# Single 32-bit matmuls in place of three half-precision passes, in three stages of a spectral filter

## The chip, the cores and the metric

The kernel runs on one core of one Trainium2 chip. The metric is the device time of one execution, in microseconds (us). The engines are TensorE (PE in the profile; its weight loads are listed apart as PEld), VectorE (DVE), ScalarE (ACT), GpSimd (POOL) and SyncE (SP), which here issues all DMAs.

## The reference

```python
x = A_x                                        # 1 x 2048 x 512, float32
xn = layernorm(x)                              # over the 512
X = rfft2(xn) * (w_r + 1j * w_i)               # 2048 x 257
s = irfft2(X, (2048, 512))
gate, up = xn @ W_gate, xn @ W_up              # 512 x 1376 each
h = gate * (gate > 0) * up
g = silu(h @ W_down)                           # 1376 x 512
return x + s * g
```

Two branches share the normalised input: a two-dimensional spectral filter, and a gated feed-forward network whose result multiplies the filter's.

## The kernel before

**Numbers in halves.** TensorE is fed in half precision. To keep the accuracy, each float32 operand is split in two fp16 numbers: a high half, written by a copy (mostly ScalarE), and a low half, the float32 value less the high half (a subtraction on VectorE). A product is then three passes into the same PSUM accumulator, high x high, high x low and low x high; `PASSES = ((0, 0), (0, 1), (1, 0))` lists the pairs. Constants are split on the host by `_half`.

**The feed-forward branch.** The 2048 rows are handled in four blocks of 512 (numbered 0 to 3), the 1376 hidden columns in eleven tiles of 128 (the last has 96), numbered `f` = 0 to 10. Gate and up product are `gu{block}_{f}_{0|1}`: four parts of the contraction by three passes, 12 matmuls of 512 columns each. `r`, `h32` and `h16` are the rectified gate, the product and its halves; `dn` are the down products, matmuls of `h16` with the scaled down weights `wds`, also in three passes, into four accumulators per block. The weights are scaled to powers of two on the chip. For gate and up that goes by groups of tiles: `squares` sums the weights' squares into `m{g}`, a small 32-bit matmul `sum{g}` with a matrix of ones (lines 507 to 515) adds them over the partitions, and VectorE makes the scales `p{g}` and their inverses `rho`. For the down weights, `down_scale` (579 to 599) multiplies `md`, the sums of absolute values in each row of a tile, with `rho`, so it needs the inverses of all seven groups, reduces them, and hands them to `greatest` (561 to 569): one DMA writes the 128 values, one per partition, to DRAM (`row_md`), a second spreads them to all partitions (`rows_md`), VectorE takes the maximum `max_md`, and five small operations (`pd`, `cdi`, `scd`) make the scales. `down_weights` (601 to 608) then writes the high half of each `wds` on ScalarE and the low half on VectorE. The filter's weights go through the same chain as `mw`.

**The filter branch.** The transform over the 512 columns is a set of folds on VectorE (sums and differences of mirrored columns, result `xs`) with matmuls by the constants `cD`; that over the 2048 rows is factored in 64 x 32. There are eight chunks of the work, and these TensorE stages:

- *First stage*, one step `s1_c` for each of the eight row chunks (`first_stage`, 462 to 484): products of the folded input `xs` with 64 x 64 matrices `cR`. Four 64 x 64 tiles of the array work side by side (two blocks of rows by two of columns). Columns 0 to 256 use one matrix and 257 to 511 another (`RANGES`), so a step is 2 ranges x 3 passes x 4 tiles = 24 matmuls. Ahead of it, `split` (454 to 460) makes the halves `xs16`. Behind it, ScalarE and VectorE write the result's halves `t1` in two pieces (448 and 64 columns) and SP stores them in DRAM (`A_d`).
- *Middle*, for each of eight chunks `q` of frequencies (`fft_chunk`, 775 to 932): `y` (64-row matmuls with the chunk's matrices `cm`), `x` (with `cD`), the multiplication by the filter on VectorE and GpSimd, `z` (with `cD`) and `v`, the inverse with 64 x 64 matrices, here called the inverse 16-point stage. `v_stage` (914 to 925) has 3 passes x 4 tiles of 512 columns; chunk 0 has three more matmuls of 255 columns with the correction matrices `cX`. Its input is split in halves in `z16`, its output in `t9`, which goes to DRAM (`C_d`).
- *Last stage*, one step `s2_c` for each of eight chunks (`last_stage`, 935 to 982): `cR[2 + m]` times the rows of `C_d`, with tiles and ranges as in the first stage, then unfolding, the product with the gate `g`, the addition of `x` and the store.

**What sets the order.** Nothing is issued as it is written. Every piece of work is a `step` (101 to 118) with an engine, a planned cost, the names that it reads and writes, and perhaps a due time. `Plan.run` (120 to 207) plays these steps through with the planned costs: on each engine it takes, among the steps that could begin about then, the one with the earliest due time. It counts buffers of each pool and a planned lag after each engine, and on TensorE it prefers steps of the same array shape (`mode`). The order in which the steps begin in this plan becomes each engine's order of instructions, fixed at build time; on the chip, semaphores hold an instruction until its inputs are there. Planned costs of the three stages are `SCOST` (first and last) and `VCOST` (inverse), line 38:

```python
YCOST, VCOST, SCOST, MODE, JOIN = 0.63, 0.59, 0.6, 0.095, 21.31
```

The small sums `sum2` to `sum6`, the accumulators of `s1`, `s2`, `y`, `x`, `z` and `v` all share one PSUM tag, `F`, of two buffers, so a third step must wait until the readers of the first are done. Nearly every operation passes through the wrapper `InOrder` (line 65), so rows of the profile carry L65 and are told apart by tile names.

Of the kernel before, what the change touches and what calls it, by code (L numbers as in the profile page):

```python
# [14 lines left out]
P = 128  # L15
# [22 lines left out]
YCOST, VCOST, SCOST, MODE, JOIN = 0.63, 0.59, 0.6, 0.095, 21.31  # L38
# [196 lines left out]
def kernel(ctx: ExitStack, tc: tile.TileContext, x, wg, wu, wd, wl, ew, sp, c_r, c_d, c_m, c_x, c_s, out):  # L235
# [12 lines left out]
    C_d = dram.tile([N1, N2, 2 * D], F16, name="C_d")  # L248
# [205 lines left out]
    def split(c):  # L454
        tile_of(f"xs16_{c}", "k4", [P, 2, 2, D], F16)
        x16, xs = (lambda: T[f"xs16_{c}"]), (lambda: T[f"xs{c}"])
        parts = [(f"xs{c}", i) for i in range(6)]
        step("ACT", act(1024), lambda: ACT.activation(x16()[:, :, 0, :], xs(), AF.Copy), reads=parts, writes=[(f"xs16_{c}", 0)])
        step("DVE", dve(1024), lambda: DVE.tensor_sub(x16()[:, :, 1, :], xs(), x16()[:, :, 0, :]),
             reads=[*parts, (f"xs16_{c}", 0)], writes=[(f"xs16_{c}", 1)], port=True)  # L460

    def first_stage(c, due):
        tile_of(f"s1_{c}", "F", [P, 2, D], F32)
        tile_of(f"t1_{c}", "k4", [P, 2, 2, D], F16)
        ps, t1 = (lambda: T[f"s1_{c}"]), (lambda: T[f"t1_{c}"])

        def run():
            x16 = T[f"xs16_{c}"]
# [6 lines left out]
        step("PE", SCOST, run, mode=1, reads=["cR", (f"xs16_{c}", 0), (f"xs16_{c}", 1)], writes=[f"s1_{c}"], due=due, margin=MARGIN)  # L475
# [299 lines left out]
    def fft_chunk(q, due):  # L775
        a16n, xsn, pfn, pon, p16n, z16n, t9n, atn, wtn = (f"{k}_{q}" for k in ("a16", "xsp", "pf", "po", "p16", "z16", "t9", "at", "wt"))
        for n, tag, shape, dtype in ((atn, "k4", [P, 2, 2, D], F16), (f"cm{q}", "k2", [P, 2, 2, 2, 64], F16),
# [5 lines left out]
                                     (z16n, "k4", [P, 2, 2, D], F16), (f"v{q}", "F", [P, 2, D], F32),  # L783
                                     (t9n, "k4", [P, 2, 2, D], F16), *((f"tt{i}_{q}", "k2", [P, 16, 32], F32) for i in range(4))):
# [21 lines left out]
        def y_stage():  # L806
            y = T[f"y{q}"]
            for b in range(2):
                for t in range(4):
                    for n, (h, l) in enumerate(PASSES):  # L810
                        for g in range(2):
# [5 lines left out]
                            matmul(y[:, g, t, b, :], at()[rows, b, h, t * P:(t + 1) * P], cm()[rows, b, 0, l, :], start=n == 0, stop=n == 2)  # L817
# [92 lines left out]
        step("ACT", act(1024), lambda: ACT.activation(z16()[:, 0], zv(), AF.Copy), reads=[f"z{q}"], writes=[(z16n, 0)])  # L910
        step("DVE", dve(1024), lambda: DVE.tensor_sub(z16()[:, 1], zv(), z16()[:, 0]), reads=[f"z{q}", (z16n, 0)], writes=[(z16n, 1)])


        def v_stage():
            v = T[f"v{q}"]
            for n, (h, l) in enumerate(PASSES):
                if n == 2 and q == 0:
                    lo, hi, _ = RANGES[1]
                    for h1, l1 in PASSES:
                        matmul(v[0:64, 0, lo:hi], cX[:, 1, h1, :], z16()[0:64, l1, 0, lo:hi], start=False, stop=False)  # L920
                for b in range(2):
                    for t in range(2):
                        at = slice(64 * t, 64 * t + 64)
                        matmul(v[64 * b:64 * b + 64, t, :], cm()[at, b, 1, h, :], z16()[at, l, b, :], start=n == 0, stop=n == 2)
        step("PE", VCOST, v_stage, mode=1, reads=[(z16n, 0), (z16n, 1), f"cm{q}", "cX"], writes=[f"v{q}"], due=due[3], margin=MARGIN)
        t9 = lambda: T[t9n]
        step("ACT", act(1024), lambda: ACT.activation(t9()[:, :, 0, :], T[f"v{q}"], AF.Copy), reads=[f"v{q}"], writes=[(t9n, 0)], due=due[3] + 4)
        step("DVE", dve(1024), lambda: DVE.tensor_sub(t9()[:, :, 1, :], T[f"v{q}"], t9()[:, :, 0, :]), reads=[f"v{q}", (t9n, 0)], writes=[(t9n, 1)], due=due[3] + 6)
        for b in range(2):
            step("SP", .6, lambda b=b: SP.dma_start(C_d[8 * q + 4 * b:8 * q + 4 * b + 4].rearrange("(t o) n x -> (o n) t x", t=2),  # L930
                                                     t9()[64 * b:64 * b + 64].rearrange("m t h d -> m t (h d)")),
                 reads=[(t9n, 0), (t9n, 1)], writes=[("C_d", q, b)], kb=256)


    def last_stage(c, due):
        ctn, zn, aen, yen, sn = (f"{k}{c}" for k in ("ct", "zz", "ae", "ye", "sv"))
        for n, tag, shape, dtype in ((ctn, "k4", [P, 2, 2, D], F16), (f"s2_{c}", "F", [P, 2, D], F32), (zn, "k4", [P, 2, D], F32),
                                     (aen, "k2", [P, 2, 2, 130], F32), (yen, "k4", [P, 2, 2, 258], F32), (sn, "k4", [P, 2, D], F32)):
            tile_of(n, tag, shape, dtype)
        for i in range(2):  # L940
            step("SP", .6, lambda i=i: SP.dma_start(T[ctn][64 * i:64 * i + 64].rearrange("s e h d -> s e (h d)"), C_r[2 * c + i]),
                 reads=[("C_d", q, b) for q in range(NCH) for b in range(2)], writes=[(ctn, i)], lead=14, kb=256)

        def run():
            for a, b, m in RANGES:
                for n, (h, l) in enumerate(PASSES):
                    for i in range(2):
                        rows = slice(64 * i, 64 * i + 64)
                        for e in range(2):
                            matmul(T[f"s2_{c}"][64 * e:64 * e + 64, i, a:b], cR[rows, 2 + m, h, :], T[ctn][rows, e, l, a:b], start=n == 0, stop=n == 2)  # L950
# [50 lines left out]
    step("SP", .6, lambda: SP.dma_start(cX, c_x), writes=["cX"], lead=20, kb=128)  # L1001
# [75 lines left out]

def _constants():
# [49 lines left out]
    c_m = _half(m2.transpose(0, 2, 1, 3, 4))  # L1128
    c_x = _half(np.stack([dM.reshape(N1, N1), dMi.reshape(N1, N1)], axis=1))
# [17 lines left out]
    return np.tile(_half(R.transpose(1, 0, 2)), (2, 1, 1, 1)), _half(dd), c_m, c_x, c_s, ks_of  # L1147
# [42 lines left out]
```

## Time and profile before

| | |
|---|---|
| device time, median of 3 runs | 408.8 us (408.79 to 408.81) |
| the profiled execution's own span | 407.1 us, 7606 instructions |
| TensorE busy | 401.4 us, 2992 matmul records |
| weight loads | 211.5 us |
| VectorE busy | 304.0 us |
| ScalarE busy | 188.0 us |
| GpSimd busy | 46.7 us |
| DMA | 51.78 MB, mean 127 GB/s |

The span is the time from the profile's first instruction to its last; the device time also has the little that lies around it. In a row, names such as `s<-xs,cR` give the written and the read tiles without their buffer numbers; `x48` counts instructions; a shape such as `64*64` ahead of the operands is the part of the array that a matmul uses. A wait row gives the waiting engine and tile, the engine and tile waited for, the total in us and the number of waits.

### The profile page before, as it was taken

To read this page: it belongs to the slowest core of one execution; us is meant where nothing else is said; L and a number is where in the kernel's file an instruction comes from. 1 tells how busy PE (TensorE), PEld (TensorE's weight loads), DVE (VectorE), ACT (ScalarE), POOL (GpSimd) and SP (SyncE) were. 2 spreads that over 40 slices of the span, in tenths; PEclk is the share of its full clock that TensorE was granted. 3 is DMA by queue.
4 is the path that set the end of the run, shared out by engine and by line. 5 is a ranking of instruction groups with operands and counts; after the bars stand their busy time and mean duration, and the time that the engine had idled before them with its cause. 6 is when DMAs were issued, how large, how long until landed. Compare 5 with 4: busy or idle time off the path is not lost.

```text
span 407.1 us, 7606 instructions
## 1 busy us (share of the span) xinstructions
PE 401.4 (99%) x2992; PEld 211.5 (52%) x2992; DVE 304.0 (75%) x647; ACT 188.0 (46%) x358; POOL 46.7 (11%) x72
## 2 busy tenths in 40 slices
PE   8999999999999999999999999999999999999995
PEld 7864444444444445455465455546555444444555
DVE  4897986998798979706987578686792328987974
ACT  4999823743467636222355433534523336242411
POOL 0000000000000000001612032030330008040300
PEclk9999999999999999999999999999999999999999
DMA  7980002218549608690006540324201297563242
GB/s 244 403 304 1 0 2 109 54 52 208 171 152 305 172 15 209 128 291 13 2 0 191 173 144 0 100 92 149 52 2 52 61 242 182 161 185 105 103 156 103
DMA packets 36291, 51.78 MB, mean 127 GB/s; under 512 B 15840, under 2 KB 17600, under 8 KB 36256
## 3 DMA queue, kind: packets, MB, share of 16 engines
q1 hardware_dynamic: 36256, 51.31, 42.5%
q8 instruction: 23, 0.38, 0.4%
q14 instruction: 12, 0.10, 0.1%
HBM read 35.55 MB, written 12.60 MB: 118 GB/s over the span
## 4 chain that ended last, share of the span: by engine, by line
PE 97%; ACT 1%; DVE 1%; issue 0%
PE gu L65 55%; PE dn L65 27%; PE s L65 3%; PE z L65 3%; PE xx L65 3%; PE small L65 2%; PE y L65 2%; PE v L65 2%; PE dn_3b L65 1%; ACT xT L65 1%; ACT wgu L65 0%; PE head L65 0%; DVE xT L65 0%; PE sum L65 0%; DVE p L65 0%
## 5 line engine op out<-in xcount | busy, mean ns | idle before, releaser
L65 PE MATMUL gu<-xT,wgu 128*128 128x512 f16 (+1 forms) x1008 | 213.3, 369 | 0.4 <-DVE xT L65 0.4
L65 PEld LDWEIGHTS <-wgu 128*128 128x128 f16 x1008 | 97.5, 98 | 107.5 <-issue 3.5
L65 PE MATMUL dn<-wds,h 128*128 128x512 f16 (+2 forms) x528 | 115.8, 373 | 0.0
L65 PEld LDWEIGHTS <-h 128*128 128x128 f16 (+1 forms) x561 | 53.7, 98 | 57.3 <-issue 2.0
L65 DVE TENSOR_TENSOR h<-gu,r 128x512 f32<-128x512 f32 (+2 forms) x52 | 33.6, 646 | 24.2 <-PE gu L65 22.9
L65 ACT ACTIVATE h<-h 128x512 f16<-128x512 f32 (+1 forms) x44 | 27.5, 626 | 51.0 <-DVE h L65 51.0
L65 POOL TENSOR_TENSOR po<-tt,tt 128x256 f32<-128x256 f32 x16 | 14.4, 900 | 262.6 <-DVE tt L65 208.7
L65 ACT ACTIVATE r<-gu 128x512 f32<-128x512 f32 (+1 forms) x44 | 26.2, 595 | 36.5 <-PE gu L65 36.3
L65 DVE TENSOR_TENSOR h<-h,h 128x512 f16<-128x512 f32 (+1 forms) x44 | 29.7, 689 | 5.3 <-ACT h L65 5.1
L65 DVE SCALAR_TENSOR_TENSOR tt<-xsp,cw,wt 128x512 f32<-128x512 f32 x32 | 25.3, 847 | 0.0
L65 POOL TENSOR_TENSOR ae<-zz 128x128 f32<-128x128 f32 (+1 forms) x32 | 17.8, 593 | 62.8 <-ACT zz L65 47.9
L65 ACT ACTIVATE g<-dn,cdi 128x512 f32<-128x512 f32 (+1 forms) x16 | 10.6, 673 | 23.9 <-PE dn L65 23.9
L65 PE MATMUL gu<-xT,wgt 128*64 128x256 f16 (+1 forms) x144 | 17.0, 309 | 0.0
L65 DVE TENSOR_TENSOR sv<-sv,g 128x512 f32<-128x512 f32 (+1 forms) x17 | 11.2, 690 | 6.4 <-ACT g L65 6.1
L65 DVE TENSOR_TENSOR t<-v,t 128x1024 f16<-128x1024 f32 x8 | 9.8, 1219 | 7.9 <-ACT t L65 7.9
L65 DVE TENSOR_TENSOR z<-z,z 128x1024 f16<-128x1024 f32 x8 | 9.7, 1218 | 7.5 <-ACT z L65 7.5
L65 ACT ACTIVATE z<-z 128x1024 f16<-128x1024 f32 x8 | 8.2, 1024 | 15.2 <-PE z L65 15.2
L65 POOL TENSOR_TENSOR pf<-tt,tt 128x256 f32<-128x256 f32 x16 | 14.0, 888 | 7.7 <-PE gu L65 7.7
L65 ACT ACTIVATE p<-pf 128x1024 f16<-128x1024 f32 x8 | 8.4, 1056 | 13.0 <-DVE pf L65 13.0
L65 DVE SCALAR_TENSOR_TENSOR wgu<-raw,p,wgu 128x512 f16<-128x512 f32 x20 | 14.4, 745 | 0.1
L65 ACT ACTIVATE xs<-xs 128x1024 f16<-128x1024 f32 x8 | 8.3, 1052 | 12.8 <-DVE xs L65 9.3
L65 ACT ACTIVATE wgu<-raw 128x512 f16<-128x512 f32 x20 | 12.3, 619 | 3.7 <-DMA raw<-in_wg 3.7
(134 smaller groups left out, 430.6 us busy)
## 6 DMA issues: line engine op xcount, KB each, us to landing
A_d<-t SPq DMA_DIRECT2D x16, 256.0 KB, 3.3
rw<-in_wl SPq DMA_DIRECT2D x8, 512.0 KB, 5.1
wt<-in_wl SPq DMA_DIRECT2D x8, 512.0 KB, 4.8
at<-A_d SPq DMA_DIRECT2D x8, 512.0 KB, 4.9
C_d<-t SPq DMA_DIRECT2D x16, 256.0 KB, 3.3
ct<-C_d SPq DMA_DIRECT2D x16, 256.0 KB, 5.6
xt<-in_x SPq DMA_DIRECT2D x16, 256.0 KB, 4.3
out<-xt SPq DMA_DIRECT2D x15, 256.0 KB, 2.1
```

The costliest lines, as they stand in the source:

```text
L65: return lambda *args, **kw: self.tc.keep_in_program_order(f(*args, **kw))
```

## The change

In the first, the inverse and the last stage, each product of three fp16 passes becomes one matmul with float32 operands. The constants `cR` are kept in float32 (one 64 x 64 matrix, 256 bytes a row, in place of two halves), and `cm` and `cX` as well, except that the half of each which the forward stage `y` uses still holds packed fp16 halves, read through a bitcast view. The inputs are no longer split: `split` returns at once and the first stage reads `xs`; `z16` and `t9` are float32 copies from PSUM, without the subtraction for a low half, and `C_d` in DRAM holds one float32 in place of two fp16. The forward intermediate `A_d` and all other products stay in halves. The planned costs of the three stages are set to .82 and .80.

```diff
-YCOST, VCOST, SCOST, MODE, JOIN = 0.63, 0.59, 0.6, 0.095, 21.31
+YCOST, VCOST, SCOST, MODE, JOIN = 0.63, 0.8, 0.82, 0.095, 21.31
...
-    C_d = dram.tile([N1, N2, 2 * D], F16, name="C_d")
+    C_d = dram.tile([N1, N2, D], F32, name="C_d")
...
-    cR = cpool.tile([P, 4, 2, N1], F16, name="cR")
+    cR = cpool.tile([P, 4, N1], F32, name="cR")
...
-    cX = cpool.tile([64, 2, 2, 64], F16, name="cX")
+    cXf = cpool.tile([64, 2, 64], F32, name="cX")
+    cX = cXf.bitcast(F16).rearrange("p a (h x) -> p a h x", h=2)
...
     def split(c):
-        tile_of(f"xs16_{c}", "k4", [P, 2, 2, D], F16)
+        return
...
             for a, b, m in RANGES:
-                for n, (h, l) in enumerate(PASSES):
-                    for e in range(2):
-                        rows = slice(64 * e, 64 * e + 64)
-                        for i in range(2):
-                            matmul(ps()[64 * i:64 * i + 64, e, a:b], cR[rows, m, h, :], x16[rows, i, l, a:b], start=n == 0, stop=n == 2)
+                for e in range(2):
+                    rows = slice(64 * e, 64 * e + 64)
+                    for i in range(2):
+                        matmul(ps()[64 * i:64 * i + 64, e, a:b], cR[rows, m, :], xs[rows, i, a:b], start=True, stop=True)
...
-                            matmul(y[:, g, t, b, :], at()[rows, b, h, t * P:(t + 1) * P], cm()[rows, b, 0, l, :], start=n == 0, stop=n == 2)
+                            matmul(y[:, g, t, b, :], at()[rows, b, h, t * P:(t + 1) * P], cm()[:, b, 0].bitcast(F16)[rows, 64 * l:64 * l + 64], start=n == 0, stop=n == 2)
...
-        step("ACT", act(1024), lambda: ACT.activation(z16()[:, 0], zv(), AF.Copy), reads=[f"z{q}"], writes=[(z16n, 0)])
-        step("DVE", dve(1024), lambda: DVE.tensor_sub(z16()[:, 1], zv(), z16()[:, 0]), reads=[f"z{q}", (z16n, 0)], writes=[(z16n, 1)])
+        step("ACT", act(1024), lambda: ACT.activation(z16(), zv(), AF.Copy), reads=[f"z{q}"], writes=[(z16n, 0)])
...
+            for b in range(2):
+                for t in range(2):
+                    at = slice(64 * t, 64 * t + 64)
+                    matmul(v[64 * b:64 * b + 64, t, :], cm()[at, b, 1, :], z16()[at, b, :], start=True, stop=bool(q or t or b))
+                    if q == t == b == 0:
+                        lo, hi, _ = RANGES[1]
+                        matmul(v[0:64, 0, lo:hi], cXf[:, 1, :], z16()[0:64, 0, lo:hi], start=False, stop=True)
...
-        step("ACT", act(1024), lambda: ACT.activation(t9()[:, :, 0, :], T[f"v{q}"], AF.Copy), reads=[f"v{q}"], writes=[(t9n, 0)], due=due[3] + 4)
-        step("DVE", dve(1024), lambda: DVE.tensor_sub(t9()[:, :, 1, :], T[f"v{q}"], t9()[:, :, 0, :]), reads=[f"v{q}", (t9n, 0)], writes=[(t9n, 1)], due=due[3] + 6)
+        step("ACT", act(1024), lambda: ACT.activation(t9(), T[f"v{q}"], AF.Copy), reads=[f"v{q}"], writes=[(t9n, 0)], due=due[3] + 4)
...
-                            matmul(T[f"s2_{c}"][64 * e:64 * e + 64, i, a:b], cR[rows, 2 + m, h, :], T[ctn][rows, e, l, a:b], start=n == 0, stop=n == 2)
+                        matmul(T[f"s2_{c}"][64 * e:64 * e + 64, i, a:b], cR[rows, 2 + m, :], T[ctn][rows, e, a:b], start=True, stop=True)
```

Since the plan is played through with other steps and other costs, the order of instructions moves too, from about a tenth of the program on. Three places matter for what follows.

**The sums of the weights' squares, on TensorE.** The rows are from the first feed-forward block; `m5` and `m6` are the sums of the last two groups of weights, `wgu4` and `wgu5` gate and up weights. Before, at the end of `gu0_4_1`:

```order
L65 MATMUL gu0_4_1_605<-xT0_233,wgu3_80 128x512
L65 MATMUL sum5_629<-m5_498,ones_94 128x4
L65 MATMUL sum6_633<-m6_547,ones_94 128x4
L65 LDWEIGHTS wgu4_81
L65 MATMUL gu0_5_1_635<-xT0_233,wgu4_81 128x512
```

Now, at the end of `gu0_7_1`:

```order
L65 LDWEIGHTS wgu5_82
L65 MATMUL gu0_7_1_742<-xT0_233,wgu5_82 128x512
L65 MATMUL sum6_758<-m6_547,ones_94 128x4
L65 LDWEIGHTS wgu5_82
L65 MATMUL gu0_8_0_760<-xT0_233,wgu5_82 128x512
```

`sum5` and `sum6` stood together ahead of `gu0_5_1`. Now six products (`gu0_5_1`, `gu0_5_0`, `gu0_6_0`, `gu0_6_1`, `gu0_7_0`, `gu0_7_1`) precede `sum6`, and `sum5` stands between two of them.

**From the maxima to the scales, on VectorE.** Before, the last operations of `p6` and `rho` and the reduction of `md`:

```order
L65 TENSOR_SCALAR p6_686<-p6_686 128x4
L65 SCALAR_TENSOR_TENSOR rho_86<-p6_686 128x2
L65 SCALAR_TENSOR_TENSOR wgu5_82<-raw5_1_393,p5_659 128x4x128
L65 TENSOR_TENSOR md_90<-md_90,rho_86 128x11
L65 TENSOR_REDUCE md_90<-md_90 128x1
```

Now:

```order
L65 TENSOR_SCALAR p6_773<-sum6_758 128x4
L65 TENSOR_SCALAR p6_773<-p6_773 128x4 x3
L65 SCALAR_TENSOR_TENSOR rho_86<-p6_773 128x2
L65 TENSOR_TENSOR md_90<-md_90,rho_86 128x11
L65 TENSOR_REDUCE md_90<-md_90 128x1
```

The chain from `sum6` to the reduction is now one uninterrupted piece. Later in the same queue come the maximum, the scales and the first `wds`. Before:

```order
L65 TENSOR_REDUCE max_md_105<-rows_md_104 128x1
L65 TENSOR_SCALAR pd_106<-max_md_105 128x1
L65 TENSOR_SCALAR pd_106<-pd_106 128x1 x2
L65 TENSOR_SCALAR cdi_87<-pd_106 128x1
L65 TENSOR_SCALAR scd_91<-rho_86,pd_106 128x11
L65 TENSOR_TENSOR xs16_1_684<-xs1_570,xs16_1_684 128x2x512
L65 TENSOR_TENSOR h32_0_8_843<-gu0_8_1_803,r0_8_817 128x512
L65 SCALAR_TENSOR_TENSOR wds_85<-wds_85,scd_91 128x512
```

Now:

```order
L65 TENSOR_TENSOR t1_0_880<-s1_0_860,t1_0_880 128x2x448
L65 TENSOR_REDUCE max_md_105<-rows_md_104 128x1
L65 TENSOR_TENSOR t1_0_880<-s1_0_860,t1_0_880 128x2x64
L65 TENSOR_SCALAR pd_106<-max_md_105 128x1
L65 TENSOR_SCALAR pd_106<-pd_106 128x1 x2
L65 TENSOR_SCALAR cdi_87<-pd_106 128x1
L65 TENSOR_SCALAR scd_91<-rho_86,pd_106 128x11
L65 TENSOR_TENSOR h16_0_9_899<-h32_0_9_869,h16_0_9_899 128x512
L65 SCALAR_TENSOR_TENSOR wds_85<-wds_85,scd_91 128x512
```

The subtractions of `t1_0` stand here now; before, they stood seventeen rows behind the maximum. On SP the two DMAs of `md` stood next to each other, and now the loads of `x2` and `x3` are issued between them.

**The last three steps of the first stage, on VectorE.** These subtractions are the last readers of the PSUM buffers of `s1_5`, `s1_6` and `s1_7`. Before:

```order
L65 TENSOR_TENSOR t1_5_1867<-s1_5_1819,t1_5_1867 128x2x448
L65 TENSOR_TENSOR t1_5_1867<-s1_5_1819,t1_5_1867 128x2x64
L65 TENSOR_TENSOR h32_1_8_1888<-gu1_8_1_1848,r1_8_1811 128x512
L65 TENSOR_SCALAR pw_113<-max_mw_112 128x1
L65 TENSOR_SCALAR pw_113<-pw_113 128x1 x3
```

Now:

```order
L65 TENSOR_REDUCE max_mw_112<-rows_mw_111 128x1
L65 TENSOR_TENSOR x16_6_1509<-xf6_1504,x16_6_1509 128x512
L65 TENSOR_SCALAR pw_113<-max_mw_112 128x1
L65 TENSOR_SCALAR pw_113<-pw_113 128x1 x3
L65 COPY cw_88<-pw_113 128x1
L65 TENSOR_TENSOR cw_88<-pw_113,cS_75 128x1
L65 TENSOR_SCALAR cwi_89<-pw_113 128x1
L65 TENSOR_TENSOR t1_5_1719<-s1_5_1696,t1_5_1719 128x2x448
L65 TENSOR_TENSOR t1_6_1741<-s1_6_1708,t1_6_1741 128x2x448
L65 TENSOR_TENSOR t1_5_1719<-s1_5_1696,t1_5_1719 128x2x64
L65 TENSOR_TENSOR t1_6_1741<-s1_6_1708,t1_6_1741 128x2x64
```

Before, `s1_5` ran alone on TensorE, and `s1_6` and `s1_7` as a pair two products later. Now `s1_5` and `s1_6` are the pair, and `s1_7` follows after one product (`gu1_8_0`) and six `dn` matmuls; on VectorE the maximum of `mw` and its small operations, which stood behind the reads of `s1_5`, stand ahead of them.

More of the change, by code (lines that the diff above doesn't have):

```diff
@@ L945, in run @@
             for a, b, m in RANGES:
[L946 to L949, printed above, removed]
-                            matmul(T[f"s2_{c}"][64 * e:64 * e + 64, i, a:b], cR[rows, 2 + m, h, :], T[ctn][rows, e, l, a:b], start=n == 0, stop=n == 2)
+                for i in range(2):
+                    rows = slice(64 * i, 64 * i + 64)
+                    for e in range(2):
+                        matmul(T[f"s2_{c}"][64 * e:64 * e + 64, i, a:b], cR[rows, 2 + m, :], T[ctn][rows, e, a:b], start=True, stop=True)
         step("PE", SCOST, run, mode=1, reads=[(ctn, 0), (ctn, 1), "cR"], writes=[f"s2_{c}"], due=due, margin=MARGIN)
@@ L1075, in _half, with _packed @@
     return np.stack([hi, lo], axis=-2)
+def _packed(a):
+    import numpy as np
+    out = a.astype(np.float32)
+    half = np.ascontiguousarray(_half(a[..., 0, :])).view(np.float32)
+    out[..., 0, :] = half.reshape(*a.shape[:-2], -1)
+    return out
 def _constants():
```

37 lines of the change are left out of this document (14 added, 23 removed).

## The prediction

> **What bounds the kernel now.** I read the page first: span, busy shares, clock, chain. Its columns are busy time and share of the span.
>
> ```profile
> span 407.1 us, 7606 instructions
> ...
> PE 401.4 (99%) x2992; PEld 211.5 (52%) x2992; DVE 304.0 (75%) x647; ACT 188.0 (46%) x358; POOL 46.7 (11%) x72
> ...
> PEclk9999999999999999999999999999999999999999
> ...
> PE 97%; ACT 1%; DVE 1%; issue 0%
> ```
>
> TensorE works in 99% of the span, at the full clock in every slice, and 97% of the chain that ended last is its own. Next I asked what TensorE waits for:
>
> ```profile
> PE small L65 <- DVE md L65: 1.1, 1, 1.1
> PE gu L65 <- DVE xT L65: 0.4, 1, 0.4
> ```
>
> Two waits, 1.5 us in all, both in the first 21 us. So what the change takes from VectorE and ScalarE is worth nothing as long as TensorE does not wait for them, and what it adds to TensorE lengthens the span one for one. A busy engine may still run below its rate, so I looked at its rows in time (start, length, engine, operation):
>
> ```profile
> 42.00 26.06 PE L65 MATMUL gu<-xT,wgu 128*128 128x512 f16 x120
> 67.99 1.51 PE L65 MATMUL s<-xs,cR 64*64 64x257 f16 x48
> 69.44 4.20 PE L65 MATMUL gu<-xT,wgt 128*128 128x512 f16 x36
> 73.56 2.76 PE L65 MATMUL dn<-wds,h 128*128 128x512 f16 x12
> ```
>
> 120 matmuls of 512 columns start between 42.00 and 67.99: 0.2166 us for 512 columns. The two first-stage steps take 69.44 - 67.99 = 1.45 us. One step is three passes over 257 + 255 = 512 columns, with four 64x64 matmuls side by side; 2 x 3 x 0.2166 = 1.30, so it runs at full column rate, and 0.15 us is the price of one visit to the small array shape.
>
> The profiled execution has a span of 407.1 us and the median of the runs is 408.8; the 1.7 us around the span are carried over unchanged, and all differences below are added to 408.8.
>
> **Part 1: the matmuls.** How many column times does a 32-bit matmul need? Rows with f32 operands exist, though none with wide moving data in an ordinary matmul:
>
> ```profile
> L65 PE MATMUL sum<-m,ones x10: 169/252/253, 15.3 to 41.9; 128*128 128x4 f32 x8, 128*128 128x2 f32 x2
> 17.30 1.04 PE L65 MATMUL head<-unit,xf 128*128 128x128 f32 x8
> ```
>
> The program has five `sum` matmuls and the trace ten records, so one 32-bit matmul is two passes. The eight f32 transposes start over 1.04 - 0.27 (the length of the last) = 0.77 us, 0.110 us each for 128 columns, which in half precision would be 128/512 x 0.2166 = 0.054: two column times per f32 column. A transpose also loads 128 weights, which may be what takes the 0.110, so this is an upper bound and the lower one is a single column time. Two passes of two make four column times against three now; two passes of one make two. I take four, from the nearest row.
>
> The Trainium skill, "FP8 and Floating Point Precision", section TensorE Precision Notes, says true FP32 is four passes, high and low half against high and low half. By that rule the sum is the one that I take; the rows alone would also allow two.
>
> A step of any of the three stages covers 512 columns with four tiles, so each of the 8 + 8 + 8 = 24 steps grows by one pass of 0.2166: **+5.2 us**. The first inverse step also has its correction on one tile alone:
>
> ```profile
> 212.37 0.27 PE L65 MATMUL v<-z,cX 64*64 64x255 f16 x1
> 212.38 0.41 PE L65 MATMUL v<-z,cm 64*64 64x512 f16 x3
> 212.48 0.38 PE L65 MATMUL v<-z,cX 64*64 64x255 f16 x2
> ```
>
> Three of 255 columns become one of four column times: **+0.1**. In the new order TensorE visits the small shapes (s, v, y) 21 times, not 22: **-0.15**.
>
> The first weights of a visit are not loaded behind earlier matmuls. What one load takes:
>
> ```profile
> L65 PEld LDWEIGHTS <-wgu 128*128 128x128 f16 x1008 | 97.5, 98 | 107.5 <-issue 3.5
> ...
> L65 PEld LDWEIGHTS head<-unit,xf 128*128 128x128 f32 x16 | 1.8, 141 | 0.0
> L65 PEld LDWEIGHTS sum<-m,ones 128*128 128x128 f32 x10 | 1.6, 191 | 0.3
> ```
>
> An f32 load is 43 to 93 ns longer than one in half precision. Eighteen visits begin or hold s or v work: 0 if it hides, 18 x 0.09 = 1.6 if not. I take the nearer, shorter difference, 0.04 each: **+0.7**. Inside a step a pass streams 0.22 or 0.43 us, which covers the load of the next.
>
> **Part 2: what goes.** Three subtractions on VectorE and one copy on ScalarE per chunk:
>
> ```profile
> L65 DVE TENSOR_TENSOR t<-v,t 128x1024 f16<-128x1024 f32 x8 | 9.8, 1219 | 7.9 <-ACT t L65 7.9
> L65 DVE TENSOR_TENSOR z<-z,z 128x1024 f16<-128x1024 f32 x8 | 9.7, 1218 | 7.5 <-ACT z L65 7.5
> L65 ACT ACTIVATE z<-z 128x1024 f16<-128x1024 f32 x8 | 8.2, 1024 | 15.2 <-PE z L65 15.2
> ...
> L65 ACT ACTIVATE xs<-xs 128x1024 f16<-128x1024 f32 x8 | 8.3, 1052 | 12.8 <-DVE xs L65 9.3 <-DVE x L65 3.5
> ```
>
> The third subtraction, that of the folded input xs, has the shape of the other two: 24 x 1.22 = 29 us off VectorE, and 8.3 us of copies off ScalarE (the copy of z stays, in 32 bits). TensorE waited for none of it, so I count **0**. If there were a gain, it could be no more than the 1.5 us of waits above, and these lie before the first of these steps. The DMAs keep their bytes (two halves or one word); the 64-column moving operands of the forward stage are the same bytes read through another view: 0.
>
> **Part 3: what moves.** Both waits below come from the new order; nothing in the edit asks for them.
>
> First, the scale of the down projection. The weight maxima go through `sum6`, a reduction, and two small DMAs, before any `wds` can be scaled:
>
> ```profile
> 50.03 0.16 DVE L65 TENSOR_REDUCE md<-md 128x1 f32<-128x11 f32 x1
> 50.22 0.33 SPq L65 DMA_DIRECT2D row_md<-md  x1
> 59.47 0.32 SPq L65 DMA_DIRECT2D rows_md<-row_md  x1
> 59.88 0.86 SPq L65 DMA_DIRECT2D x<-in_x  x2
> 64.45 0.29 DVE L65 TENSOR_REDUCE max_md<-rows_md 128x1 f32<-128x128 f32 x1 [4.16 <-DMA rows_md<-row_md]
> 65.61 0.72 ACT L65 ACTIVATE wds<-wds,scd 128x512 f16<-128x512 f32 x1 [4.62 <-DVE scd L65]
> 67.22 0.74 DVE L65 SCALAR_TENSOR_TENSOR wds<-wds,scd 128x512 f16<-128x512 f32 x1
> ```
>
> From the reduction to the maximum it is 14.4 us, 9.25 of them for the first DMA. Today the first `wds` is whole at 67.96 and needed at 73.56: 5.6 us spare. In the new order `sum6` stands behind gu0_7_1, six products later on TensorE. A product is 12 x 0.2166 = 2.6 us; from 42.00, where gu0_5_1 starts now (less the 0.2 or so of one small sum that moves with it), that is 57.4. Its last pass ends 0.25 later (252 ns above), and seven small VectorE operations, each like the one at 50.03, take about 1.2: the reduction ends at 58.9, 8.7 later than now. On SP the two loads of x now stand between the two small DMAs; they are issued in 0.86 us while the first of these flies, so they cost nothing. The maximum comes at 73.15. One more subtraction of 0.28 stands between it and the scales, so ScalarE starts the first `wds` at 65.61 + 8.7 + 0.28 = 74.6 and has the high half at 75.3; VectorE needs its 0.74 for the low half: 76.05. TensorE gets to dn0_0 at 73.56 + 0.43 (two longer steps) = 74.0. Its first matmul waits 1.3 for the high half, the second 0.6 for the low one: **+1.9**. Between later `wds` VectorE has one or two other operations, while the new order gives TensorE 6 or 12 matmuls (1.3 or 2.6 us) for each, so only the first costs. The lower bound comes from the sister chain:
>
> ```profile
> 141.09 0.33 SPq L65 DMA_DIRECT2D row_mw<-mw  x1
> ...
> 148.39 0.32 SPq L65 DMA_DIRECT2D rows_mw<-row_mw  x1
> ```
>
> The same DMA took 7.3 there; 1.95 less leaves 0.05. I keep the md chain's own row, so 1.9, with 0 and 2.5 as ends.
>
> Second, s1_7. Three first-stage steps share two PSUM buffers. In the new order s1_5 and s1_6 run as a pair, then one product (2.6) and six dn (1.3), then s1_7, which needs the buffer of s1_5. How long a pair holds its first buffer:
>
> ```profile
> 158.81 1.60 PE L65 MATMUL s<-xs,cR 64*64 64x257 f16 x48
> ...
> 164.14 1.49 DVE L65 TENSOR_TENSOR t<-s,t 128x896 f16<-128x896 f32 x3 [0.51 <-ACT t L65]
> ```
>
> The pair ends at 160.4, and the second of these three subtractions, the last reader of the first buffer, ends near 165.4: 5.0 us later. s1_7 comes after 2.6 + 1.3 + 0.16 = 4.1: **+0.9**. Behind it on TensorE stands everything. Bounds: 0, and 2.9 if `row_mw`, whose maximum now stands ahead of these subtractions on VectorE, takes 9.25 instead of 7.3.
>
> The inverse stage comes 3.5 us or more behind its z stage, and needs one ScalarE copy of 1.0 us now: no wait. The end (gate, two VectorE operations, store) is as before.
>
> **The sum:** 5.2 + 0.1 - 0.15 + 0.7 + 1.9 + 0.9 = +8.65, so 408.8 + 8.65 = **417.5 us**.
>
> **Rivals.**
> *A, passes that block each other (443 us).* If matmuls start strictly in program order, the second pass of a matmul waits for the first on the same tile and holds up the next matmul, which could have run on another. Eight matmuls then take nine slots of 0.2166 (1.95, not 0.65), and the inverse stage's four take five of 0.433 (2.17): 16 x 1.30 + 8 x 1.52 = +32.9, with the first wait gone, since TensorE comes late itself: 408.8 + 32.9 + 0.9 + 0.6. Against it: in the rows of the first inverse step above, three `cm` matmuls start at 212.38, ahead of the second and third `cX` (212.48), which stand before them in the code. The Trainium skill, "TensorE: Matmul & The Clock Gate", Part 3, says that matmuls are strict FIFO in start and end. By that rule this rival holds; the trace has starts out of order by 0.1 us, and the measurement decides. For it: no f32 matmul of the trace sits in a small tile. 10%.
>
> *B, two column times (408.0 us): the other side.* If a pass takes one column time per column, a step needs two passes of 0.2166, not three: 24 x -0.2166 = -5.2. TensorE is then earlier at dn0_0 by 0.87, so that wait grows to 2.8. -5.2 + 2.8 + 0.9 + 0.1 + 0.7 - 0.15 = -0.85. It decides for faster below about 1.1 column times per pass. Only the weight loads of the transposes speak for it. 8%.
>
> *C, the waits do not come (414.6 us).* The small DMA takes 7.3, and VectorE gets to s1_5's subtractions 1 us earlier, having 29 us less to do: +5.2 + 0.1 - 0.15 + 0.7. 15%.
>
> **How the numbers follow.** The forecast has 67%. Its low end is C without load cost, 413.9; its high end 5.3 + 1.6 + 2.5 + 2.9 - 0.15 = +12.15, 420.9. From 413.5 to 421 the range takes in the forecast and C, 82%. A measurement of this kernel can tell about 0.2% from no change. Faster by more than that: half of B, 4%; within: the other half, 4%, since B stands right at that line; slower: 92%.
>
> **What would show it.** f32 rows of `s` and `v` starting four at a time, every 0.22 us (s) and 0.43 us (v), so that the visit of s1_0 and s1_1 takes about 1.9 us, not 1.45. A wait of TensorE of about 2 us for `wds` near 74 us, and one of about 1 us before s1_7 near 160. VectorE busy about 275 us. I am wrong if the starts of different tiles are spaced by a whole pass (A), if that visit takes about 1.1 us (B), or if TensorE shows waits at other places, which would be an order that I have misjudged.

## The result and the profile after

| | before | after |
|---|---|---|
| device time, median of 4 runs | 408.8 us | 427.15 us (425.44 to 427.74) |
| ratio | | 1.0439, 95% interval 1.0418 to 1.0460 |
| span of the profiled execution | 407.1 us | 423.6 us |
| TensorE waits | 1.5 us | 8.7 us |
| VectorE busy | 304.0 us | 281.5 us |

The changed kernel is 4.4% slower, by 18.3 us at the median, where 8.65 was forecast. The sign was right and the size was not: the time lies outside the range given. The page of the changed kernel, with the lines that answer to those of before:

```profile
span 423.6 us, 7258 instructions
...
PE 410.9 (97%) x2831; PEld 211.4 (50%) x2831; DVE 281.5 (66%) x623; ACT 180.3 (43%) x350; POOL 47.8 (11%) x72
...
PEclk9999999899999989999999999999999999999999
...
PE 89%; DVE 5%; DMA 2%; ACT 2%; issue 1%; SPq 0%; DVEq 0%; ACTq 0%
```

Two things are new beside the longer work of TensorE. The chain that ended last now runs through VectorE, DMAs and ScalarE for some 9% of the span, and two slices have less than the full clock. The waits of TensorE (total in us, number, longest):

```profile
PE gu L65 <- DVE h L65: 3.5, 1, 3.5
PE dn L65 <- ACT wds L65: 3.1, 1, 3.1
PE small L65 <- DVE md L65: 1.1, 1, 1.1
PE dn L65 <- DVE wds L65: 0.4, 1, 0.4
PE gu L65 <- DVE xT L65: 0.4, 1, 0.4
PE s L65 <- DVE t L65: 0.2, 1, 0.2
```

The third and the fifth are those of before. The others, in TensorE's rows in time (start, length, and the wait ahead in brackets):

```profile
68.16 1.96 PE L65 MATMUL s<-xs,cR 64*64 64x257 f32 x32
70.05 4.20 PE L65 MATMUL gu<-xT,wgt 128*128 128x512 f16 x36
77.30 0.38 PE L65 MATMUL dn<-wds,h 128*128 128x512 f16 x1 [3.05 <-ACT wds L65]
...
156.50 4.44 PE L65 MATMUL gu<-xT,wgu 128*128 128x512 f16 x12 [3.46 <-DVE h L65]
160.86 1.96 PE L65 MATMUL s<-xs,cR 64*64 64x257 f32 x32
162.76 2.76 PE L65 MATMUL gu<-xT,wgu 128*128 128x512 f16 x12
```

The wait for `wds` was forecast, at 74.25 and with 1.9 us; it is 3.05 and then 0.41. The wait before 156.50 (it is `gu1_7_1`) was not forecast at all. The twelve matmuls behind it take 4.36 us to the next row instead of 2.6. The windows of four us that have less than the full clock (TensorE busy, clock, DMA share, GB/s), in the order of time:

```profile
76.00:80.00 4.00, 2.29 (x6) 0.76 0.53 135
80.00:84.00 4.00, 4.00 (x16) 0.81 0.01 2
...
156.00:160.00 4.00, 3.50 (x9) 0.57 0.14 12
```

Behind each of the two long waits the clock is low: 4 x 0.24 + 4 x 0.19 = 1.7 us lost at the first, 4 x 0.43 = 1.7 at the second. So the 16.5 us between the two profiled executions are: 5.7 for the longer matmuls (experiment 1 measures this alone), 3.05 + 0.41 + 3.46 + 0.20 = 7.1 of new waits, 3.4 of half rate; 0.3 stays unexplained. The median of the timed runs lies 1.7 above the profiled one. One more half-rate stretch would be of that size, but it would lower the mean granted clock by 0.004, and the two runs at 427.15 and 427.16 us have 0.990 against 0.991 in the profiled one; so that is unlikely, and what these 1.7 us are stays open.

Why do the waits come? At the first place SP issues the two loads of `x` between the small store `row_md` and its read-back:

```profile
59.29 0.33 SPq L65 DMA_DIRECT2D row_md<-md  x1
59.71 0.86 SPq L65 DMA_DIRECT2D x<-in_x  x2
69.33 0.33 SPq L65 DMA_DIRECT2D rows_md<-row_md  x1
```

and VectorE, in its fixed order, meets the first use of `x2` ahead of everything that leads to the scales:

```profile
64.02 1.28 DVE L65 TENSOR_TENSOR h<-h,h 128x512 f16<-128x512 f32 x2
70.45 0.70 DVE L65 BATCH_NORM_STATS2 st<-x 128x6 f32<-128x512 f32 x1 [5.14 <-DMA x<-in_x]
...
74.27 1.07 DVE L65 TENSOR_TENSOR t<-s,t 128x896 f16<-128x896 f32 x1
75.26 0.28 DVE L65 TENSOR_REDUCE max_md<-rows_md 128x1 f32<-128x128 f32 x1
```

The loads land 10.7 us after their issue (59.71 to 70.45). `rows_md` itself took 3.0 us and was there at 72.3, but the maximum had to wait in VectorE's queue until 75.26. At the second place the same small store of the filter's chain stands between the two stores of `t1_4`:

```profile
145.36 0.55 SPq L65 DMA_DIRECT2D A_d<-t  x1
145.96 0.59 SPq L65 DMA_DIRECT2D row_mw<-mw  x1
146.59 0.68 SPq L65 DMA_DIRECT2D A_d<-t  x1
154.17 0.32 SPq L65 DMA_DIRECT2D rows_mw<-row_mw  x1
```

Before, both stores of `t1_4` were issued ahead of `row_mw` (141.09), and no store of `t1` behind it until 159.48. The second of `t1_4`:

```profile
139.02 1.33 SPq L65 DMA_DIRECT2D A_d<-t  x1
```

Now VectorE needs the storage buffer of `t1_4` for the last folds (`xs`), and only then reaches the `h` that frees TensorE's PSUM buffer:

```profile
148.70 0.49 DVE L65 TENSOR_TENSOR xs<-ee 128x130 f32<-128x130 f32 x2
155.42 0.43 DVE L65 TENSOR_TENSOR xs<-eo 128x256 f32<-128x256 f32 x1 [6.22 <-DMA A_d<-t]
155.76 0.68 DVE L65 TENSOR_TENSOR h<-gu,r 128x512 f32<-128x512 f32 x1
```

The theory that the experiments test (theory 1): the matmuls cost one column time more; all the rest comes from the new order, in which big transfers stand behind the two small stores of 128 x 4 bytes, and are finished only with them; a TensorE wait of some 3 us then also costs a stretch at half rate. The rivals: the 32-bit matmuls lower the clock or stall by themselves; the late `sum6` alone makes the first wait; VectorE is late for its work and not for a transfer.

### The profile page after: what moved, and what is told of

The parts are those of the page before. It is cut to its first block, busy times and chain, and to the rows that moved or that the text cites. A ratio compares the mean times of both kernels' runs of the same rounds, so it can differ in the third digit from the quotient of the medians.

```text
span 423.6 us, 7258 instructions
## 1 busy us (share of the span) xinstructions
PE 410.9 (97%) x2831; PEld 211.4 (50%) x2831; DVE 281.5 (66%) x623; ACT 180.3 (43%) x350; POOL 47.8 (11%) x72
## 4 chain that ended last, share of the span: by engine, by line
PE 89%; DVE 5%; DMA 2%; ACT 2%; issue 1%; SPq 0%; DVEq 0%; ACTq 0%
PE gu L65 48%; PE dn L65 26%; PE s L65 3%; PE z L65 3%; PE xx L65 2%; PE small L65 2%; DMA A_d<-t 2%; PE v L65 2%; PE y L65 2%; DVE t L65 1%; DVE h L65 1%; PE dn_3b L65 1%; DVE eo L65 1%; ACT xT L65 1%; ACT junk L65 0%
## 5 line engine op out<-in xcount | busy, mean ns | idle before, releaser
L65 PE MATMUL dn<-wds,h 128*128 128x512 f16 (+2 forms) x528 | 117.9, 376 | 3.5 <-ACT wds L65 3.1
L65 POOL TENSOR_TENSOR po<-tt,tt 128x256 f32<-128x256 f32 x16 | 15.5, 967 | 287.4 <-ACT xo L65 193.6
L65 ACT ACTIVATE g<-dn,cdi 128x512 f32<-128x512 f32 (+1 forms) x16 | 10.6, 672 | 18.3 <-PE dn L65 18.3
L65 DVE TENSOR_TENSOR xsp<-xx,xo 128x256 f32<-128x256 f32 (+1 forms) x16 | 5.0, 351 | 19.3 <-ACT xsp L65 17.5
L65 ACT ACTIVATE t<-s 128x896 f16<-128x896 f32 (+1 forms) x16 | 8.7, 592 | 17.9 <-PE s L65 15.9
L65 DVE TENSOR_TENSOR pf<-po 128x128 f32<-128x128 f32 x32 | 15.5, 539 | 0.6 <-POOL po L65 0.6
L65 DVE BATCH_NORM_STATS2 st<-x 128x6 f32<-128x512 f32 x16 | 10.8, 672 | 7.5 <-DMA x<-in_x 7.5
L65 ACT ACTIVATE t<-v 128x1024 f32<-128x1024 f32 x8 | 8.2, 1024 | 17.7 <-PE v L65 15.5
L65 DVE TENSOR_TENSOR t<-s,t 128x896 f16<-128x896 f32 (+1 forms) x16 | 10.4, 682 | 7.1 <-ACT t L65 7.0
L65 DVE TENSOR_TENSOR p<-pf,p 128x1024 f16<-128x1024 f32 x8 | 9.8, 1224 | 8.0 <-ACT p L65 8.0
```

Of the source, the lines that this page charges most:

```text
L65: return lambda *args, **kw: self.tc.keep_in_program_order(f(*args, **kw))
```

## The experiments

All ratios are to the kernel before on the same chip, with 95% intervals; the rows come from one profiled execution each.

**1. The old order.** The dropped steps stay in the plan, with the old costs, and issue nothing:

```diff
-YCOST, VCOST, SCOST, MODE, JOIN = 0.63, 0.8, 0.82, 0.095, 21.31
+YCOST, VCOST, SCOST, MODE, JOIN = 0.63, 0.59, 0.6, 0.095, 21.31
...
+        step("DVE", dve(1024), lambda: None, reads=[f"z{q}", (z16n, 0)], writes=[(z16n, 1)])
```

> The changed kernel, but planned with the steps and the costs of before: the dropped copies and subtractions stay in the plan as steps that issue nothing, so every engine has the order of before with the dropped instructions missing. Theory 1 (the 32-bit matmuls cost one more column time per column, all the rest of the loss is order): no new wait of TensorE over 0.5 us, full clock, 408.8 + 24 x 0.2166 + 0.1 = 414.1 us. Rival (the 32-bit matmuls lower the clock or stall by themselves): the granted clock stays near 0.99 and the time stays over 420. With 0.7 for weight loads, as forecast, 414.8.

Measured: 414.3 us, ratio 1.0143 (1.0128 to 1.0158). Its span, and all waits of TensorE:

```profile
span 412.8 us, 7271 instructions
...
PE small L65 <- DVE md L65: 1.1, 1, 1.1
PE gu L65 <- DVE xT L65: 0.4, 1, 0.4
```

Only the waits of before are left, and the clock is full throughout. The same 32-bit matmuls in the old order cost 5.7 us of span; 24 x 0.2166 = 5.2 of it are column times, and the correction and the weight loads share the other 0.5. Two thirds of the loss are order.

**2. The loads of x ahead of `row_md`**, the rest as changed. After the planner has sorted its steps, the two are moved:

```diff
+        for moved, before in [(('x2', 0), 'row_md'), (('x3', 0), 'row_md')]:
+            k = next(i for i, (_, s) in enumerate(order) if moved in s.names and s.engine == "SP")
+            o = order.pop(k)
+            order.insert(next(i for i, (_, s) in enumerate(order) if before in s.names and s.engine == "SP"), o)
```

> The changed kernel, with only the loads of x2 and x3 moved on SP from behind the store row_md to ahead of it. Theory 1 (transfers that are issued behind the 128 x 4-byte store land only with it, and VectorE, waiting for x2, is late for the scales): the loads land in some 4 us, VectorE no longer waits 5 us for them, the maximum comes near 72.5 instead of 75.26, the wait at the first dn falls from 3.46 to 0.7 to 1.5 us, and the half-rate stretch behind it goes: 427.2 less 3.7 to 4.5 = 422.7 to 423.5. Rival 1 (the late sum6 alone makes the wait, the place of the loads is of no account): 427 with 3.4 us of wait. Rival 2 (my forecast's sum: wait of 1.9, no slow stretch): 423.9.

Measured: 422.2 us, ratio 1.0338 (1.0322 to 1.0353), clock 0.994. VectorE and SP at the place:

```profile
64.94 0.69 DVE L65 BATCH_NORM_STATS2 st<-x 128x6 f32<-128x512 f32 x1
...
71.35 0.29 DVE L65 TENSOR_REDUCE max_md<-rows_md 128x1 f32<-128x128 f32 x1
```

```profile
59.00 0.33 SPq L65 DMA_DIRECT2D row_md<-md  x1
66.58 0.32 SPq L65 DMA_DIRECT2D rows_md<-row_md  x1
```

`sum6` is as late as in the changed kernel, yet TensorE does not wait for `wds` at all, not even the 1.9 us of the forecast. The maximum comes 3.9 us earlier, at 71.35: 2.9 of them are VectorE's own queue, since in the changed kernel the values were there at 72.3, and about 1.0 are the two small DMAs. From the issue of the store to the landing of the read-back these took 12.3 us here (7.6 and 4.7), 13.0 in the changed kernel and 14.2 in the row that the forecast used. Rival 1 falls. The other wait grew to 4.5 us, since TensorE came earlier, and a new one of 1.6 us for the first `at<-A_d` of the middle part appeared: 3.46 + 1.7 left, 1.1 + 1.6 came, and the span is 2.8 shorter. The time is a little below the range expected.

**3. The second store of `t1_4` ahead of `row_mw`**, moved in the same way (`[(('A_d', 4, 1), 'row_mw')]`).

> The changed kernel, with only the second store of t1_4 to A_d moved on SP from behind the store row_mw to ahead of it. Theory 1: the store lands some 4 us after its issue instead of 8.7, VectorE no longer waits 6.2 us for its buffer, the wait of 3.46 us before gu1_7_1 and its half-rate stretch of 1.7 go, and 0.5 to 1.5 us of wait come back at s1_7: 427.2 - 5.2 + 0.3 to 1.3 = 422.3 to 423.3. Rival (VectorE is late there for its work, not for the transfer): 426 to 427.

Measured: 424.9 us, ratio 1.0395 (1.0360 to 1.0429). The wait before `gu1_7_1` is gone, so the rival about VectorE's work falls, but the time is above the range expected and the four runs spread (422.9 to 425.7): `s1_7` now waits 2.57 us, and in the profiled execution the first wait was longer, with `row_md` issued at 59.15 and its read-back only at 70.47.

```profile
PE dn L65 <- ACT wds L65: 4.8, 1, 4.8
PE s L65 <- DVE t L65: 2.6, 1, 2.6
```

**4. Both moves.**

> The changed kernel with both moves. Theory 1: the gains add up, 427.2 - 4.1 - 4.4 = 418.7 (417.5 to 419.7), clock 1.0 throughout. Rival (one stall was hiding the other, or a third one appears): 421 or more.

Measured: 418.1 us, ratio 1.0241 (1.0226 to 1.0256), clock 1.0 in the profiled execution (0.993 to 0.996 in the three others, which took as long to within 0.9 us). The time is as expected, but it is not the sum of the two measured gains: alone the moves lower the ratio by 0.0101 and 0.0044, about 4.1 and 1.8 us, and together by 0.0198, about 8.1. Each move alone leaves the other stall in place, and longer (4.5 and 4.8 + 0.4 us, against 3.46 both times). The interval of experiment 3 alone is 1.4 us to each side. What is left over experiment 1 is 416.2 - 412.8 = 3.4 us of span, and two waits make it: 2.24 at `s1_7` and 1.12 at the first `at<-A_d`. The chain of waits ahead of `s1_7`, in order of time (start, length, what):

```profile
141.43 7.97 DMA row_mw<-mw
...
149.41 4.33 DMA rows_mw<-row_mw
...
153.77 0.29 DVE max_mw L65
...
156.98 1.30 DVE t L65 x2
...
158.41 1.09 PE s L65 x16
```

**5. As 4, and `max_mw` behind the reads of `s1_5` and `s1_6`** on VectorE:

```diff
+        take = [k for k, (_, s) in enumerate(order) if s.engine == "DVE" and ("all_mw" in s.names)]
...
+        order[last + 1:last + 1] = taken
```

> Both SP moves, and on VectorE the maximum of mw with its small operations moved from ahead of the subtractions of t1_5 and t1_6 to behind them. Theory 1 (the 2.24 us before s1_7 that are left are VectorE waiting for rows_mw ahead of the last readers of the PSUM buffer): that wait goes, 7.6 us over before remain of 9.85, 415.9 (415.0 to 417.2, as the wait of 1.1 before the first y may grow). Rival (VectorE has too much to do there): 418 as without the move.

Measured: 416.1 us, ratio 1.0177 (1.0162 to 1.0193). The wait at `s1_7` is gone, as expected; 1.5 us for `at<-A_d` stay.

**6. The store made short, in the changed order.** The two small stores write 48 and 44 bytes of one partition; left out are the other 127.

```diff
-SP.dma_start(row.rearrange("a p -> p a"), col)
+SP.dma_start(row, col[0:1])
```

> The changed kernel in its own order, with the two stores row_md and row_mw of 128 x 4 bytes replaced by stores of one row of 48 or 44 bytes from one partition, and the reduction behind them over these few numbers; left out is the maximum over the other 127 partitions, so the scales are other numbers. Everything else keeps its place, the loads of x2 and x3 and the store of t1_4 behind these stores too. Theory 1 (it is the 128 small writes that hold up what is issued behind them): the store takes 2 to 4 us instead of 8 to 10, the loads and the store behind it are not late, both stalls and both half-rate stretches go: 414.1 plus 0 to 2.5 for s1_7 and y, 414.3 to 416.5. Rival (any store to DRAM with a wait for it behind takes that long, or the loads are slow for another reason): 423 or more.

Measured: 415.3 us, ratio 1.0152 (1.0137 to 1.0167). Every transfer stands where the change put it, and both stalls are gone. The store is done at most 1.3 us after its issue, when its read-back goes out:

```profile
59.21 0.29 SPq L65 DMA_DIRECT2D row_md<-md  x1
59.60 0.81 SPq L65 DMA_DIRECT2D x<-in_x  x2
60.50 0.38 SPq L65 DMA_DIRECT2D rows_md<-row_md  x1
```

**7 and 8. Which edit moves the order?** Experiment 7 sets back the two planned costs alone (the diff's first line in experiment 1); experiment 8 keeps the new costs and leaves the dropped steps in the plan (its second).

> The changed kernel with the planned costs of before (0.59 and 0.6), the steps dropped as in the change. If the dropped steps move the order: the stall for wds stays (3 to 5 us, with 1.7 of half rate), the one before gu1_7_1 goes since the order differs there, s1_7 waits some 2.3: 414.1 + 5 to 7 + 2 = 421 to 424. If the new costs move it: order of before, 414 to 415.

> The changed kernel with its own planned costs, but with the dropped copies and subtractions left in the plan as steps that issue nothing. If the dropped steps move the order: only waits of 0.9 and twice 0.3 at later dn matmuls, no half rate: 415.3 (414.3 to 416.5). If the new costs move it: 420 or more.

Measured: 424.5 us (423.0 to 426.1), ratio 1.0394 (1.0354 to 1.0433), with a first wait of 3.7 and 1.1 us, for experiment 7; 414.9 us, ratio 1.0148 (1.0132 to 1.0163), waits 0.2 beyond those of before, for experiment 8. Dropping the steps brings the costly order; the new costs alone, in experiment 8, do not. They have a part in it all the same: with the old costs there is no wait before `gu1_7_1`, as the second store of `t1_4` is then issued ahead of `row_mw`. So the first stall comes from the dropped steps whatever the costs, the second only with both edits. With the dropped steps in the plan, `row_md` is issued at 50.15, as before, and the loads of x at 60.15, behind its read-back.

**9. No 32-bit matmul, in the changed order.** A single bf16 pass over the upper halves; left out is the lower half of each operand.

```diff
+def top(a):
+    return a.bitcast(BF)[:, 1::2]
...
-                        matmul(ps()[64 * i:64 * i + 64, e, a:b], cR[rows, m, :], xs[rows, i, a:b], start=True, stop=True)
+                        matmul(ps()[64 * i:64 * i + 64, e, a:b], top(cR[rows, m, :]), top(xs[rows, i, a:b]), start=True, stop=True)
```

> The changed kernel in its own order, with every 32-bit matmul replaced by a single bf16 pass over the upper halves of the same numbers; left out is the lower half of both operands. No 32-bit matmul is left in the three stages, and a step has one column time instead of four. If the order makes the stalls and a stall of 3 us makes the half rate: TensorE comes 1.3 us earlier to the first dn and waits 4 to 5 us there, waits 3.5 to 5 us before gu1_7_1, and both times runs some 3.4 us at half rate; 408.8 - 24 x 0.433 + 9 + 3.4 + 0 to 2 for s1_7 and y = 410.8 to 412.8, clock near 0.99. Rival (32-bit matmuls bring the low clock or the stalls): full clock, 398 to 402.

Measured: 417.3 us, ratio 1.0198 (1.0174 to 1.0223), clock 0.983. Slower than before, although each step has two passes fewer than there:

```profile
78.86 0.59 PE L71 MATMUL dn<-wds,h 128*128 128x512 f16 x1 [6.33 <-ACT wds L71]
79.65 28.92 PE L71 MATMUL dn<-wds,h 128*128 128x512 f16 x125 [0.20 <-DVE wds L71]
158.15 4.53 PE L71 MATMUL gu<-xT,wgu 128*128 128x512 f16 x12 [5.44 <-DVE h L71]
```

Stalls and half rate are there without any 32-bit matmul in these stages, so the rival about the matmuls falls. The expectation was 4.5 to 6.5 us too low. The two long waits were 6.5 and 5.4 us, and with those at `s1_7` (1.3) and for `at<-A_d` (1.4) the new ones come to 14.6, where 9 to 11 were expected: TensorE came earlier, and the transfers did not.

**10 and 11. What is slow in the store?** In 10 the 128 values go to addresses 512 bytes apart; in 11 each is written as a row of 512 bytes. Both read back only the first value; the maximum over the others is left out.

```diff
-        row = dram.tile([1, P], F32, name=f"row_{name}")
+        row = dram.tile([P, P], F32, name=f"row_{name}")
...
-SP.dma_start(row.rearrange("a p -> p a"), col)
+SP.dma_start(row[:, 0:1], col)
```

> The changed kernel with the 128 x 4-byte stores spread in DRAM: one value every 512 bytes instead of side by side; only the first value is read back, left out is the maximum over the others. If the stores are slow since all 128 small writes fall in one 512-byte stretch: store and loads behind it take 2 to 4 us, no stall, 414.3 to 416.5. If 128 small writes are slow wherever they go: still 8 to 10 us for the store, x2 and x3 land 10 us after their issue, 422 to 427.

> The changed kernel with each of the 128 values written 128 times, so that the store is 128 rows of 512 bytes (64 KB) instead of 128 x 4 bytes; only the first value is read back, left out is the maximum over the others; one small ScalarE copy ahead of each store is added. If it is small writes that hold the queue up, this store takes 2 to 4 us and nothing behind it is late: 414.3 to 416.5. If it is the wait for any store to DRAM: 422 to 427.

Measured: 415.3 us, ratio 1.0156 (1.0135 to 1.0176), and 415.4, ratio 1.0158 (1.0137 to 1.0178), from two runs each. No new wait over 0.4 us in either. The DMA rate from 59 to 75 us in forty slices of 0.4 us, first of the changed kernel, then of experiment 10; in both the loads of x are issued at 59.7 to 59.8, right behind the store:

```profile
GB/s 0 0 1 1 102 41 102 205 195 72 92 0 41 31 20 31 41 20 20 10 31 20 51 61 41 51 287 379 379 234 165 42 19 0 0 0 0 0 0 0
```

```profile
GB/s 0 0 0 1 92 82 184 379 410 399 440 410 206 21 0 0 0 0 0 0 0 0 0 0 0 0 0 0 0 0 0 0 0 0 0 82 220 184 159 292
```

Above, the loads run at 41 to 205 GB/s for some 3 us, then crawl, mostly at 10 to 60, until the store is done at 69.3, and then run at up to 379. Below, they move in 4 us (what comes at 73 us is a store of `t1`). The number of small writes and their size are the same in both; what differs in the store is that they lie side by side in 512 bytes, or apart.

**12. A version that is faster than both.** The kernel before, in its own order, with the first of its three passes alone in the three stages; left out are the products with a low half, so these stages have the precision of fp16.

```diff
+HIGH = ((0, 0),)
...
-                for n, (h, l) in enumerate(PASSES):
+                for n, (h, l) in enumerate(HIGH):
```

> The kernel before, in its own plan, with one fp16 pass (high half x high half) instead of three in the same three stages; left out are the two products with a low half, so these stages have the precision of fp16. If the price of the stages is column times and nothing else, and the old order leaves no wait: 408.8 - 24 x 0.433 - 0.4 for the correction of the first inverse step = 398.0 us, and up to 3 more if TensorE, earlier now, has to wait for VectorE near s1_5 to s1_7: 398 to 401. Rival (the order of before has as little spare as the changed one, so that an earlier TensorE stalls over 3 us and drops to half rate): 404 or more.

Measured: 399.4 us, ratio 0.9761 (0.9745 to 0.9777), clock 1.0, with 1.0 us of new waits. It is 9.5 us faster than before, where 24 x 0.433 = 10.4 of column time went. Against experiment 9, which has the same column times, the old order is worth 18 us, although the dropped copies and subtractions are still done in it. It pays with precision; at full precision none of the kernels here beats the one before.

## Why the prediction was wrong, point by point

**The matmuls: right.** 5.2 + 0.1 + 0.7 for column times, the correction and weight loads was 6.0; experiment 1 has 5.7 with the same number of visits as before. The pair s1_0, s1_1 took 70.05 - 68.16 = 1.89 us, as forecast: 2 x 4 x 0.2166 and 0.15 for the visit are 1.88. Rivals A (443 us) and B (408.0) are out: 32-bit passes on four tiles run side by side at four column times per column. The load term was too large at 0.04 a visit: with some 0.4 left beside column times and correction it is about 0.02 for each of 18 visits.

**What goes: worth nothing, as forecast.** TensorE gained nothing from it. VectorE is busy 281.5 us where about 275 was forecast: the 24 subtractions are gone with 29 us, but other rows grew, `pf<-po` most, from 11.1 to 15.5; why, no run shows. Worse, the dropped steps are what moved the plan (experiments 7 and 8).

**The wait for `wds`: the failed step.** The prediction said of the loads of x that "they are issued in 0.86 us while the first of these flies, so they cost nothing". That counts the issue and not the landing. They land 1.1 us after the store ahead of them is done, 10.7 us after their issue; VectorE waits for them 5.14 us ahead of the scales, and TensorE 3.46 instead of 1.9. The small DMAs were not the cause: they brought the values at 72.3, ahead of the 73.15 that the prediction has for the maximum, which came at 75.26. Without the loads behind the store (experiment 2) the wait is not 1.9 but 0, so the move of `sum6` costs nothing by itself there. The prediction took the longer of two measured stores, 9.25 us; the shorter, 7.3, would have given no wait (its sum has 0.05, but 1.9 less 1.95 is nothing), and experiment 2 had 7.6. Rival C, no waits at all, is out as well: its 414.6 us is what the matmuls cost in the old order (414.3 in experiment 1).

**The stall before `gu1_7_1`: missing.** It is the same mechanism at the sister store. SP's order in the changed program has `row_mw` between the two stores of `t1_4`, and the prediction followed only the md chain on SP's queue. 3.46 us. It had named waits of TensorE at other places as a sign of an order misjudged, and this is one.

**The half rate: missing.** The trace of before has no TensorE wait over 1.1 us, so nothing in it shows what a longer one costs. 2 x 1.7 = 3.4 us. The Trainium skill, "TensorE: Matmul & The Clock Gate", Part 1, says that the array's clock falls to half after an idle window of about 3.4 us and comes back after about 3.4 us of work. The rows agree on the stretch, and the waits put the limit a little lower: no half rate behind 2.24 us (experiment 4) and 2.57 (experiment 3), half rate behind 3.05 and 3.46.

**The wait at s1_7: right place, other cause.** 0.9 was forecast and 0.20 came, behind a stall in which VectorE could catch up. With the stalls gone (experiment 4) it is 2.24, within the 2.9 that was given for a slow `row_mw`. When the maximum of `mw` is moved away (experiment 5) nothing is left: the pair's own hold on its buffer, which the 0.9 stood for, cost nothing, and the maximum, which was only in the bound, made all of it.

In the sum: 5.85 forecast for the matmuls and 5.7 measured; 1.9 for `wds` against 3.46 + 1.7; 0.9 against 0.20; nothing against 3.46 + 1.7 before `gu1_7_1`.

## What to carry to other kernels

When an edit moves a transfer behind another on one queue, ask when the one ahead completes, not how long its issue takes, and follow the waits of in-order engines for the moved one; a tiny store can be the slowest of all. An engine that has time to spare still sets the order of a planned kernel: dropping its work moved waits onto TensorE, and keeping the dropped steps in the plan gave back 12 us. And count a stall of TensorE of 3.05 to 3.46 us, as here, as about 5, since the half-rate stretch behind it comes on top.

## What the hardware showed that was not expected

- A store of 128 x 4 bytes to 512 adjacent bytes of DRAM takes 7.2 (experiment 12, `row_mw`) to 11.3 us (experiment 3, `row_md`) until its read-back is issued. For `row_md` it was 10.0 to 11.3 with the loads of `x` right behind it (the changed kernel, experiments 3, 7 and 9), 7.3 to 8.0 with them ahead (experiments 2, 4 and 5). The same 128 writes laid 512 bytes apart take at most 1.5 us (59.42 to 60.88 in experiment 10):

```profile
59.42 0.33 SPq L65 DMA_DIRECT2D row_md<-md  x1
59.84 0.87 SPq L65 DMA_DIRECT2D x<-in_x  x2
60.88 0.33 SPq L65 DMA_DIRECT2D rows_md<-row_md  x1
```

- While it lasts, loads behind it run mostly at 10 to 60 GB/s, where experiment 10 has 379 to 440. Another store behind it moves its data in time and is reported late. The DMA rate of the changed kernel from 135 to 160 us in slices of 0.625 us: the stores of `t1_4`, issued at 145.36 and 146.59, have moved their bytes by 149.4 ((108 + 210 + 185 + 216 + 121) x 0.625 = 525 KB, which is two stores of 256 KB), and VectorE was released at 155.35.

```profile
GB/s 318 164 216 338 374 274 371 387 284 316 270 120 98 400 328 13 0 0 108 210 185 216 121 0 0 0 0 0 0 0 0 0 25 43 34 30 0 0 0 0
```

- The Trainium skill, "DMA: Bandwidth & Descriptors", section Queues, rings and completion order, says that a transfer's semaphore is a strongly ordered write that lands only after every earlier write of that DMA engine. The late report of a store whose data had long gone agrees with it. Why adjacent small writes take that long, no run here shows.
